# Chunk-selected attention with a gated linear unit: ten of the 32 query and key transposes moved from TensorE to DMA, and a new order

## The chip, the cores and the metric

One core of a Trainium2 chip runs the whole program. It has TensorE (matrix multiplications and transposes, into PSUM banks), VectorE, ScalarE and GpSimd for element-wise work, and SyncE (SP), which here only issues DMAs. The metric is the device time of one execution in microseconds (us); a kernel is told by the median of its runs. In the profile the engines are PE (PEld is its weight load), DVE, ACT, POOL and SP.

## The reference

The inputs are q, k and v of shape (4, 8, 768, 64), fp32, and three weights. Keys lie in 24 chunks of 32. For each query and each chunk an upper bound of the score is formed from the chunk's smallest and largest keys; the six best chunks among those not in the future are kept, and a causal softmax attention runs over them. A gated unit with a causal convolution of width 5 follows.

```python
k_min, k_max = np.min(k_chunks, axis=3), np.max(k_chunks, axis=3)
ub = np.sum(np.maximum(q[:, :, :, None, :] * k_min[:, :, None, :, :],
                       q[:, :, :, None, :] * k_max[:, :, None, :, :]), axis=-1)
ub = np.where(causal, ub, -1e9)
top_chunks = np.argsort(ub, axis=-1)[..., -6:]
scores = 0.125 * q @ k^T, masked to the chosen chunks and to pos_q >= pos_k
attn_out = softmax(scores) @ v
x = attn_out.transpose(0, 2, 1, 3).reshape(B, S, H * D)
gate = sigmoid(sum over j of conv_w[j] * x shifted by 4 - j)
out = (gate * (x @ w_val)) @ w_out
```

## The kernel before, in words

The 32 heads are worked as 16 pairs p (0 to 15); the two heads of a pair fill the 128 partitions with 64 each. Four pairs make one batch entry. Each step of a pair is a named operation in a graph; `build` (line 282) declares it with its engine, its assumed cost, what it reads and writes, and the PSUM groups it uses. The program isn't scheduled by the graph: the list `ORDER` (line 114) writes out all 1616 names in one order, with the PSUM bank after "=", and `emit_in_order` emits them so. Each engine executes its own operations strictly in that order, and so does each DMA queue; waits between engines follow from the data.

The names, for pair p and half w (384 of 768 positions):

- `Lk`, `Lq`, `Lv`: loads on SP (line 621). A key or query load is one DMA per head; pair 0 is split in two parts, so four DMAs each.
- `KT`, `QT`: three fp32 128x128 transposes on TensorE each (line 637). From PSUM, `KE` (ScalarE) casts the keys to fp16, `KX` (VectorE, four for a pair) takes maximum and minimum of each chunk, `QH` (ScalarE) casts the queries to fp16, times 16, and `QL` (VectorE) forms the fp16 rest.
- `AH`, `AL` (VectorE): |q| in two fp16 parts. `KB`, `KS` (GpSimd): the chunk bounds in fp16 parts. `KN` and `KM` don't exist before.
- `CF`, `BD` (TensorE): the bounds; `T8` (VectorE): the eight largest; `CM`: the mask; `MT` with `ME`: the mask turned on TensorE and copied, for pairs 0 to 9; `MD`: the same by one DMA transpose, for pairs 10 to 15. Pair 0 takes its bounds in fp32 instead (`KF`, `QF`, `RF`, `BF`), and all its five `BF` lie in one PSUM bank.
- `S` (TensorE): scores with the mask added; `E` (ScalarE): exp; `A` (GpSimd): the causal triangle; `VC` (GpSimd): values to fp16; `AV` (TensorE): times values; `RC`, `NR` (VectorE): normalisation.
- `XT`: the result turned for the second part, by DMA for pairs 8 to 14, by TensorE with `XTE` else; `XH` (GpSimd): the convolution's halo.
- `CV` (TensorE, for two pairs): convolution; `TH` (ScalarE): gate; `VL`, `GV`: x times w_val, times gate; `OU`, `OE`, `ST`: output matmul, eviction, store. `wval`, `wvd`, `wout` load the weights; `wvd` copies w_val to the other half of the partitions on SP's queue.
- `F`, `G`: filler matmuls at the start.

Line 640 is thus all fp32 transposes, 653 is `KX`, 647 `KE`, 682 `QH`, 721 `QL`, 728 and 731 `AH` and `AL`, 765 `BD`, 773 `T8`, 796 `MD`, 813 `S`, 838 `AV`, 862 `XT` by DMA, 902 `CV`, 917 `VL`, 923 `GV`, 931 `OU`, 939 `OE`.

Of the kernel before, what the change touches and what calls it, by code (L numbers as in the profile page):

```python
# [75 lines left out]
def emit_in_order(graph, names, nbanks=8):  # L76
# [24 lines left out]
    "dmat": set(range(8, 15)),  # L101
    "dmam": set(range(10, 16)),
# [12 lines left out]
mKF0 wval30 mfz F0=0 F1 F2 F3 F4 F5 mxT F6 F7 F8 ident identb mKB1 cfill identh mVA0 F9 F10 F11 F12  # L115
F13 Lq0.0 F14 F15 G14=1 G12 G13 G10 G11 G9 Lk0.0 KT0.0=2 KX0.00 KX0.01 QT0.0=3 G3 Lk0.1 KT0.1=4 G17
KX0.10 G6 G19 G5 RF0.0 KE0.0 G18 G7 G4 G16 KX0.11 G1 KF0.11 KF0.10 QF0.0 ident2 G2 KF0.00 KF0.01 G0
Lk1.0 KT1.0=5 KX1.01 KX1.00 KT1.1=6 KX1.11 mVA1 em0 em1 KX1.10 Lq0.1 QT0.1=7 G15 BF0.2=0 BF0.1 cwl
KE0.1 RF0.1 QF0.1 BF0.5 BF0.3 BF0.4 em2 QH0.1 Lq2.0 QT2.1=2 QT2.0=4 mNS0 mKB0 cwn1 T80.5 cwn0 cwt=7
# [59 lines left out]
E10.14 KX12.01 T811.3 S10.5=07 BD11.2 T811.2 T811.5 AV8.05 E10.05 KB12.5 AV8.03 E10.04 S10.3=54
E10.03 E10.15 E10.13 S10.0=60 E10.10 BD11.1 E10.00 AV8.00 A9.01 KB12.0 A9.03 A9.04 AV9.01=3 AV9.05  # L180
T811.4 KT13.1=5 T811.1 RC8.0 NR8.0 CM11 AV9.03 AV9.04 AV9.02 KX13.10 KX13.11 AV9.12=7 AV9.00 Lq13.0
RC9.0 NR9.0 S10.1=41 E10.11 KE13.1 AV9.10 AV9.15 E10.01 AV9.13 AV9.11 S10.2=02 E10.02 KT13.0=6
KX13.01 KX13.00 KE13.0 Lv10 wout2 VC10 E10.12 AV9.14 wvd1 MD11 CV3.0=1534 CV3.1 TH3.11 TH3.01 RC9.1
NR9.1 S11.4=06 E11.04 E11.14 AL12 VL0.0=72 GV0.01 GV0.00 A10.15 A10.03 S11.2=43 TH3.00 S11.0=06
# [55 lines left out]
def pool(n, per=0.86):  # L240
# [856 lines left out]
```

## Time and profile before

| | |
|---|---|
| median of 3 runs | 187.21 us (186.26 to 188.31) |
| profiled execution | 186.9 us, span 185.2 us |
| granted TensorE clock | 1.00 |
| busy: TensorE, ScalarE, VectorE, GpSimd | 176.5, 140.3, 125.8, 109.6 us |
| DMA queue of SP and ScalarE | 28.06 MB, 73.0% of 16 engines' span |

The span runs from the first to the last instruction. A busy share is an average over stages that have different limits. Matmuls are pipelined and their ends are modelled, so a full TensorE in a window of small matmuls needn't be full. In the rows, "x" is a count; in the groups of instructions the columns after the bar are busy time, mean duration of one in ns, and the idle time of the engine before them with what ended it. In windows, each engine's busy time is followed by its count of instructions, then the granted clock, the DMA share and GB/s. In the chain of waits the columns are start, duration, and what.

### The profile page before, as it was taken

The numbers are of one execution on the slowest core, as the hardware profiler recorded it, in microseconds if no ns is written. First come the engines' busy times: TensorE is split into PE (matmuls) and PEld (weight loads), VectorE is DVE, ScalarE is ACT, GpSimd is POOL, SyncE is SP. The second block draws the span as 40 slices with busy tenths as digits, with TensorE's granted clock in tenths as the row PEclk, the third lists the DMA queues.
The fourth block names the chain that finished last, engine by engine and source line by source line (L and its number), as shares of the span: only waits on it lengthen the run. The fifth ranks groups of instructions, "written<-read, shape, count | busy, mean of one in ns | idle before, by whom it ended". The sixth has DMA issues, their size and how long they took to land.

```text
span 185.2 us, 8893 instructions
## 1 busy us (share of the span) xinstructions
PE 176.5 (95%) x3714; PEld 127.2 (69%) x3714; DVE 125.8 (68%) x429; ACT 140.3 (76%) x320; POOL 109.6 (59%) x309
## 2 busy tenths in 40 slices
PE   7999999999999999989899999998999999999992
PEld 5696666878876787767667685786667677656441
DVE  0569999989999889998664579558923432710370
ACT  2369999999999799998698767595765979248032
POOL 7965899999999958899729423248641634100000
PEclk9999999999999999999999999999999999999999
DMA  5999989999999999960679993895047239537046
GB/s 106 213 221 217 204 189 231 193 192 229 195 210 190 211 217 199 226 122 4 144 133 178 183 209 98 178 98 151 4 81 90 69 95 173 153 119 282 8 173 224
DMA packets 89912, 29.68 MB, mean 160 GB/s; under 512 B 85387, under 2 KB 86667, under 8 KB 89872
## 3 DMA queue, kind: packets, MB, share of 16 engines
q1 hardware_dynamic: 88880, 28.06, 73.0%
q0 software_dynamic: 992, 1.06, 4.1%
q8 instruction: 29, 0.48, 1.1%
q14 instruction: 11, 0.09, 0.2%
HBM read 20.98 MB, written 6.29 MB: 147 GB/s over the span
## 4 chain that ended last, share of the span: by engine, by line
PE 59%; DVE 23%; DMA 7%; issue 3%; POOL 2%; ACT 2%; SPq 2%; DVEq 0%; POOLq 0%; ACTq 0%
PE ps L917 10%; PE ps L931 9%; DVE KK L653 8%; PE ps L902 7%; PE ps L838 7%; PE ps L810 6%; PE ps L640 6%; PE ps L813 5%; DMA vn<-in_v_dram 3%; PE ps L765 3%; DVE ON L848 3%; DVE TOP L773 3%; DMA xT<-ON 3%; DVE QL L721 2%; DVE RH L728 2%
## 5 line engine op out<-in xcount | busy, mean ns | idle before, releaser
L817 ACT ACTIVATE P<-ps 128x512 f16<-128x512 f32 (+1 forms) x192 | 89.6, 596 | 7.1 <-PE ps L813 6.6
L829 POOL TENSOR_SCALAR_AFFINE_SELECT P<-P 128x256 f16<-128x256 f16 (+1 forms) x128 | 43.6, 363 | 19.7 <-ACT P L817 18.2
L813 PE MATMUL ps<-QM,EM 64*128 64x512 f16 (+4 forms) x256 | 37.4, 290 | 0.3
L653 DVE TENSOR_REDUCE KK<-ps 128x12 f32<-128x384 f32 x64 | 32.8, 549 | 6.8 <-PE ps L640 6.4
L810 PE MATMUL ps<-QH,KE 64*128 64x512 f16 (+4 forms) x256 | 35.7, 291 | 0.0
L923 DVE SCALAR_TENSOR_TENSOR GV<-G,ps 128x384 f16<-128x384 f32 x32 | 16.3, 549 | 23.6 <-PE ps L917 23.6
L838 PE MATMUL ps<-VA,P 128*128 128x65 f16 x672 | 30.7, 194 | 0.9 <-DVE KK L653 0.6
L838 PEld LDWEIGHTS <-P 128*128 128x128 f16 x672 | 26.3, 98 | 6.5 <-issue 2.9
L917 PE MATMUL ps<-xT,wv 64*128 64x384 f16 x256 | 24.1, 323 | 0.5 <-issue 0.5
L939 ACT ACTIVATE OSB<-ps 128x512 f32<-128x512 f32 (+1 forms) x22 | 12.9, 597 | 15.0 <-PE ps L931 7.7
L931 PE MATMUL ps<-wo,GV 128*128 128x512 f16 (+1 forms) x100 | 22.9, 370 | 0.0
L773 DVE MAX8 TOP<-ps 128x8 f32<-128x16 f32 (+4 forms) x160 | 15.9, 166 | 8.3 <-PE ps L765 5.4
L907 ACT ACTIVATE G<-ps 128x384 f32<-128x384 f32 x32 | 14.0, 502 | 8.4 <-PE ps L902 8.3
L740 POOL CAST VA<-vn 128x768 f16<-128x768 f32 x16 | 14.3, 892 | 9.2 <-DMA vn<-in_v_dram 9.1
L917 PEld LDWEIGHTS <-wv 64*128 64x128 f16 x256 | 13.5, 94 | 8.8 <-issue 1.9
L647 ACT ACTIVATE KE<-ps 128x384 f16<-128x384 f32 x32 | 16.8, 564 | 2.3 <-DVE KK L653 1.5
L810 PEld LDWEIGHTS <-KE 64*128 64x128 f16 x256 | 14.0, 94 | 6.1 <-issue 1.6
L902 PE MATMUL ps<-xT,diag 32*32 32x384 f16 x1280 | 17.5, 326 | 0.6 <-issue 0.5
L848 DVE TENSOR_TENSOR ON<-ps,RCP 128x384 f16<-128x384 f32 x32 | 17.5, 553 | 0.7
L682 ACT ACTIVATE QH<-ps 128x384 f16<-128x384 f32 x32 | 15.7, 543 | 3.0 <-PE ps L640 3.0
L902 PEld LDWEIGHTS <-diag 32*32 32x32 f16 x1280 | 14.2, 88 | 3.4 <-issue 1.7
L640 PE MATMUL ps<-ident,kn 128*128 128x128 f32 x96 | 15.5, 281 | 0.3 <-DMA kn<-in_k_dram 0.3
(75 smaller groups left out, 305.7 us busy)
## 6 DMA issues: line engine op xcount, KB each, us to landing
vn<-in_v_dram SPq DMA_DIRECT2D x16, 384.0 KB, 6.3
out_dram<-OSB SPq DMA_DIRECT2D x23, 256.0 KB, 2.8
kn<-in_k_dram SPq DMA_DIRECT2D x30, 192.0 KB, 4.8
qn<-in_q_dram SPq DMA_DIRECT2D x30, 192.0 KB, 5.2
wv<-in_moe_w_val_dram POOLq DMA_DIRECT2D x8, 64.0 KB, 4.4
wo<-in_moe_w_out_dram POOLq DMA_DIRECT2D x4, 128.0 KB, 4.8
wv<-wv SPq DMA_DIRECT2D x4, 128.0 KB, 4.7
qn<-in_q_dram SPq DMA_DIRECT2D x4, 96.0 KB, 2.8
```

The source lines that it names most:

```text
L640: nc.tensor.transpose(out=pt[:, tl * 128:(tl + 1) * 128], in_=t[:, 3 * w + tl, :], identity=ident)
L653: nc.vector.tensor_reduce(out=KK[p % 2][:, mx, w * 12:(w + 1) * 12], in_=bank(gr, None).rearrange("p (c t) -> p c t", t=CH), axis=AX.X, op ...
L773: nc.vector.max(out=TOP[p % 2][:, it - 1, s, :], in_=bounds(gr)[:, it - 1, s * NCH:s * NCH + n])
L810: nc.tensor.matmul(out=pq[hh][:, col + a:col + n], lhsT=KE[p % 3][HP[hh], ks], rhs=QH[p % 3][HP[hh], q0 + a:q0 + n], start=True, stop=False)
L813: nc.tensor.matmul(out=pq[hh][:, col + a:col + n], lhsT=EM[HP[hh], ks], rhs=qm[HP[hh], q0 + a - 128:q0 + n - 128], start=False, stop=True)
L817: e.EX = lambda p, hh, bi, tot, gr: nc.scalar.activation(out=PT[hh, bi, p % 2][:, 0:tot], in_=bank(gr, None)[:, 0:tot], func=AF.Exp, scale ...
L829: nc.gpsimd.affine_select(out=ap, in_=ap, pattern=[[0, n], [1, 128]], compare_op=ALU.is_ge, fill=0.0, base=0, channel_multiplier=-1)
L838: nc.tensor.matmul(out=pav[:, qt, :], lhsT=PT[a, bi, p % 2][:, col:col + 128], rhs=VA[p % 3][:, hh, jt, :], start=(jt == 0), stop=(jt == qt))
L848: e.NR = lambda p, hh, gr: nc.vector.tensor_tensor(out=ON[(p // 2) % 2][:, 2 * (p % 2) + hh].rearrange("p t h d -> p h t d"), in0=bank(gr, ...
L902: nc.tensor.matmul(out=pc[i][os], lhsT=diag[rs, cp * NG + gi, j, :], rhs=x[rs, gi, :, a:a + 128], start=(j == 0), stop=(j == 2 * KSZ - 1), ...
L917: nc.tensor.matmul(out=pv[h], lhsT=wval_sb[HP[h], n, wc:wc + 255:2], rhs=xT[HP[h], (b % 2) * 2 + cp, gi, :, LD:LD + 128], start=(n == 0), ...
L931: nc.tensor.matmul(out=po[:, 0:z - a], lhsT=GVT[(b % 2) * NCT + et][:, s * 128:(s + 1) * 128], rhs=wout_sb[:, et, a:z], start=(et == 0), s ...
```

## The change

Four things are edited.

1. The first loads: each part of pair 0's keys and queries is issued as two DMAs of one head each on two queues, head 0 on SP (`Lk0.0` and so on), head 1 on ScalarE (`Hk0.0`).
2. The first bounds: pair 0's `BF` lie in three banks (tiles 5 and 4, 3 and 2, 1); its mask is turned in two pieces (`MT0`/`ME0` for tiles 2 to 5, `MU0`/`MV0` for tile 1). Two of the four `KF` go from ScalarE to VectorE.
3. The queries of pairs 10 to 15: `QN.0` (ScalarE) casts the loaded queries to fp16, `QN.1` (VectorE) forms the fp16 rest, and `QD.0` and `QD.1` turn both by DMA transposes on SP straight into `QH` and `QL`. `QT`, `QH` and `QL` are gone there. The keys of pairs 12 to 15: `KN.0` (ScalarE) casts, `KN.1` and `KN.2` (GpSimd) form the rest times 2048 in fp16, `KY.0` and `KY.1` turn both by DMA, `KN.3` (VectorE) adds them back to fp32, and two `KM` (VectorE) take the chunk bounds over 768 columns. `KT`, `KE` and `KX` are gone there. The fp16 parts use the memory of earlier tensors (`CW`, `QF`).
4. `ORDER` is another one (1610 names).

```diff
+    "dmaq": set(range(10, 16)),
+    "dmak": set(range(12, 16)),
...
+BGRP = {5: 0, 4: 0, 3: 1, 2: 1, 1: 2}
...
+                if nsp == 2:
+                    for hh, en in enumerate(("SP", "ACT")):
+                        g.op(en, 500, 500, "LH"[hh] + f"{what}{p}.{part}",
+                             lambda part=part, hh=hh, en=en: e.load(what, p, part, nsp, en, (hh,)), (),
+                             [(key, k4, part, "h")[:3 + hh]], dma=1800.0 / 4)
+                    continue
...
+    def QN(p, n):
+        hi, lo = QNA[:, p % 2, 0:S], QNA[:, p % 2, S:S + SELT * 128]
+        t = qn[p % 4]
+        if n == 0:
+            nc.scalar.activation(out=hi, in_=t.rearrange("p t d -> p (t d)"), func=AF.Copy, scale=QS)
+        else:
+            nc.vector.scalar_tensor_tensor(
+                out=lo, in0=t[:, 1:NT].rearrange("p t d -> p (t d)"), scalar=QS, in1=hi[:, 128:S],
+                op0=ALU.mult, op1=ALU.subtract)
+    def QD(p, n):
+        dst, src = (QL[p % 2], QNA[:, p % 2, S:S + SELT * 128]) if n else (QH[p % 3], QNA[:, p % 2, 0:S])
+        nc.sync.dma_start_transpose(out=dst.rearrange("p (t c) -> p t c", c=128), in_=src)
+    def KN(p, n):
+        t = kn[p % 4].rearrange("p t d -> p (t d)")
+        hi, lo, lot = KNA[:, 0], KNA[:, 1], KNA[:, 2]
+        if n == 0:
+            nc.scalar.activation(out=hi, in_=t, func=AF.Copy)
+        elif n == 1:
+            nc.gpsimd.tensor_tensor(out=t, in0=t, in1=hi, op=ALU.subtract)
+        elif n == 2:
+            nc.gpsimd.tensor_scalar(out=lo, in0=t, scalar1=LS, scalar2=None, op0=ALU.mult)
+        else:
+            nc.vector.scalar_tensor_tensor(out=t, in0=lot, scalar=1.0 / LS, in1=KE[p % 3],
+                                           op0=ALU.mult, op1=ALU.add)
+    def KY(p, n):
+        dst, src = (KNA[:, 2], KNA[:, 1]) if n else (KE[p % 3], KNA[:, 0])
+        nc.sync.dma_start_transpose(out=dst.rearrange("p (t c) -> p t c", c=128), in_=src)
+    e.KMx = lambda p, mx: nc.vector.tensor_reduce(
+        out=KK[p % 2][:, mx], in_=kn[p % 4].rearrange("p t (c i) -> p (t c) i", i=CH), axis=AX.X,
+        op=ALU.min if mx else ALU.max)
```

The new order of the parts that the prediction speaks of, by engine (names of other steps left out where marked):

```
SP, start:  Lk0.1 Lk0.0 Lk1.0 Lq0.1 Lq0.0 Lk2.0 Lq1.0 Lq2.0 Lk3.0 ...
ACT queue:  Hq0.0 Hq0.1 Hk0.1 Hk0.0, ahead of the first KE
VectorE, start: KX0 (4) KX1.11 KF0.11 KF0.01 KX1.00 KX1.01 T80.4 KX1.10 KX2.01 KX2.00 T80.5 KX2.11 CM0.5 T80.3 T80.2 CM0.4 CM0.3 CM0.2 KX2.10 QL1.0 T80.1 ME0 ...
SP, later:  ... QD10.0 QD11.1 Lv9 QD10.1 Lq12.0 QD11.0 Lk14.0 Lk13.0 MD10 wvd1 KY12.0 KY12.1 wvd2 wvd0 wvd3 MD11 Lq13.0 QD12.0 KY13.0 KY13.1 QD12.1 QD13.0 QD13.1 Lv10 KY14.0 KY14.1 Lq14.0 MD12 Lk15.0 Lv11 QD14.0 ST0.0 QD14.1 MD13 XT10 Lv12 KY15.0 XT11 KY15.1 XT9 XT8 MD14 ...
GpSimd:     ... wval30 KB11.3 ... A10.04 A10.15 wout0 XH7 KN13.1 KN13.2 A10.03 KB12.0 KB12.5 KB12.1 wout3 wout2 ...
TensorE:    ... CV3 VL0.0 S11.1 VL0.3 S11.5 S11.2 S11.3 VL0.1 S11.0 S11.4 VL0.2 CV7 OU0.5 OU0.0 CF12 BD12 (5) OU0.4 OU0.2 OU0.1 AV10.12 ...
```

More of the change, by code (lines that the diff above doesn't have):

```diff
@@ L114 @@
 ORDER = """
[L115 to L119, printed above, removed]
@@ L179 @@
[L179 to L184, printed above, removed]
@@ L185 @@
-TH3.10 VL0.1=12 GV0.10 E11.10 E11.00 S11.1=57 E11.01 Lk14.0 AH12 A10.14 E11.02 E11.11 A10.11 Lq14.0
-GV0.11 VL0.2=60 GV0.20 GV0.21 E11.12 KB12.1 S11.3=15 E11.13 VL0.3=24 S11.5=76 E11.05 E11.03 KS12
-KB12.2 VC11 KB12.4 A10.01 KB13.0 A10.04 A11.14 GV0.30 CF12=3 KB13.5 KB12.3 BD12.2 BD12.4 BD12.5
-KB13.1 BD12.3 T812.3 A10.13 KS13 XT7=0 XTE7 XH7 A10.05 KB13.2 KT14.1=5 KX14.10 GV0.31 T812.5 KB13.3
-QT13.1=7 QH13.1 Lv12 QL13.1 E11.15 A11.15 Lv15 QT14.0=2 QT13.0=1 QT14.1=0 KT14.0=6 KX14.01 QH13.0
-QL13.0 AL13 BD12.1 T812.2 QH14.1 QH14.0 AH14 QL14.0 KE14.0 KE14.1 Lk15.0 KB13.4 Lq15.0 AV10.05=4
@@ new lines @@
+AV9.10 AV9.14 AV9.11 KY12.0 KN13.0 CM11 A9.15 AV9.15 RC9.0 NR9.0 S10.0=35 RC9.1 NR9.1 KY12.1 KN12.3
+KM12.0 wvd2 wvd0 KM12.1 CV3.0=2104 E10.10 E10.00 wvd3 CV3.1 TH3.00 TH3.11 TH3.01 VL0.0=76 GV0.01
+GV0.00 wout1 MD11 S11.1=53 E11.01 E11.11 VL0.3=24 GV0.31 TH3.10 GV0.30 QN12.1 S11.5=06 E11.05 E11.15
+S11.2=57 E11.12 S11.3=31 E11.13 E11.03 VL0.1=04 GV0.10 GV0.11 Lq13.0 QN13.0 QN13.1 A10.04 A10.15
+QD12.0 AH12 E11.02 wout0 S11.0=62 E11.10 E11.00 S11.4=71 XH7 VL0.2=30 CV7.0=5426 CV7.1 KY13.0 KN13.1
@@ new lines @@
+KN14.0 KN13.2 A10.03 KY13.1 KN13.3 GV0.20 KB12.0 KB12.5 KB12.1 wout3 GV0.21 TH7.10 TH7.00 QD12.1
+wout2 OU0.5=3 TH7.11 TH7.01 OE0.5 A11.03 A10.14 QD13.0 QN15.0 AL12 OU0.0=0 KM13.0 KM13.1 A11.13
+OE0.0 KS12 KB12.2 E11.14 A10.13 KB12.4 CF12=4 KB12.3 BD12.4 BD12.2 BD12.1 KN14.1 KN14.2 BD12.5
+BD12.3 T812.3 OU0.4=5 OE0.4 OU0.2=6 OE0.2 OU0.1=2 OE0.1 KB13.0 KB13.5 A10.01 KB13.1 AH13 QD13.1 AL13
+Lv10 VC10 AV10.12=3 AV10.02=0 AV10.13 KS13 KB13.2 KY14.0 KB13.3 A10.05 OU0.3=1 CF13=5 KB13.4 T812.2
+T812.1 T812.5 AV10.10 BD13.2 BD13.5 BD13.3 AV10.14 T812.4 CM12 OE0.3 AV10.01 E11.04 KY14.1 KN14.3
@@ L309, in pair @@
         load("v", "vn")
-        for w in range(2):
+        if p in P["dmak"]:
+            knk = [("kn", k4, 0), ("kn", k4, 1)]
+            over = [(x, 0, w) for x in ("QF", "RF") for w in range(2)] if p == min(P["dmak"]) else []
+            c, l = act(S)
+            g.op("ACT", c, l, f"KN{p}.0", lambda: e.KN(p, 0), knk, [("KNh",)] + over, ())
+            c, l = pool(S)
+            g.op("POOL", c, l, f"KN{p}.1", lambda: e.KN(p, 1), knk + [("KNh",)], knk, ())
+            g.op("POOL", c, l, f"KN{p}.2", lambda: e.KN(p, 2), knk, [("KNl",)] + over, ())
+            g.op("SP", 1300, 1300, f"KY{p}.0", lambda: e.KY(p, 0), [("KNh",)],
+                 [("KE", k3, w) for w in range(2)], (), dma=700.0)
+            g.op("SP", 1300, 1300, f"KY{p}.1", lambda: e.KY(p, 1), [("KNl",)], [("KLO",)] + over, (),
+                 dma=700.0)
+            c, l = dve(S)
+            g.op("DVE", c, l, f"KN{p}.3", lambda: e.KN(p, 3),
+                 [("KLO",)] + [("KE", k3, w) for w in range(2)], knk, ())
+            for mx in range(2):
+                g.op("DVE", c, l, f"KM{p}.{mx}", lambda mx=mx: e.KMx(p, mx), knk,
+                     [("kk", k2, mx, w) for w in range(2)], ())
+        for w in range(2) if p not in P["dmak"] else ():
             gr = g.group()
             g.op("PE", 3 * 109, 2 * 109 + 280, f"KT{p}.{w}", lambda w=w, gr=gr: e.KT(p, w, gr),
-                 [("kn", k4, w), ("ident",)], [("kps", p, w)], [gr])
+                 [("kn", k4, w), ("kn", k4, w, "h"), ("ident",)], [("kps", p, w)], [gr])
             c, l = act(HB)
@@ L336, in pair @@
                 for n in range(2):
[L337 removed]
+                    eng = "DVE" if n else "ACT"
+                    g.op(eng, 90, 205, f"KF{p}.{hh}{n}", lambda hh=hh, n=n: e.KFb(p, hh, n), kks,
                          [("KF", k2, hh, n)], ())
@@ L381, in pair @@
              [("VA", k3)], ())
-        gr = g.group()
+        gs = [g.group() for _ in range(3 if full else 1)]
+        bg = {it: gs[BGRP[it] if full else 0] for it in range(1, NT)}
         for it in range(1, NT):
+            gr = bg[it]
             if full:
@@ L619, with load @@
     cq = {"k": (kn, k), "q": (qn, q), "v": (vn, v)}
-    def load(what, p, part, nsp, eng):
+    def load(what, p, part, nsp, eng, heads=(0, 1)):
         en = nc.sync if eng == "SP" else nc.scalar
@@ L629, in load @@
         n = NT // nsp
-        for hh in range(2):
+        for hh in heads:
             en.dma_start(
```

268 lines of the change are left out of this document (150 added, 118 removed).

## The prediction

> **What bounds the kernel now.** I read the busy time in long stretches first, then TensorE's transposes in the same stretches.
>
> ```profile
> core 0: us, PE busy (x) PEld busy (x) DVE busy (x) ACT busy (x) POOL busy (x), PEclk, DMA share, GB/s
> 0.00:20.00 20.00, 18.39 (x182) 13.90 (x183) 12.01 (x50) 12.25 (x30) 14.22 (x39) 1.00 1.10 191
> 20.00:95.00 75.00, 72.65 (x1569) 55.31 (x1568) 68.31 (x245) 70.80 (x167) 64.83 (x181) 1.00 0.94 185
> 95.00:105.00 10.00, 9.80 (x273) 6.69 (x274) 6.05 (x15) 7.80 (x17) 7.09 (x19) 1.00 0.79 144
> 105.00:180.00 75.00, 74.16 (x1689) 50.38 (x1684) 39.05 (x122) 48.04 (x107) 23.45 (x71) 1.00 0.55 125
> ...
> 95.00:105.00 10.00, 0.90 (x6) 0.42 (x5) 1.00 0.79 144
> 105.00:180.00 75.00, 3.64 (x30) 3.24 (x30) 1.00 0.55 125
> ```
>
> The first rows are all instructions by engine; the last two are line 640 alone, TensorE's fp32 transposes of keys and queries. There are three regimes. To 20 us VectorE and ScalarE are idle two fifths of the time, so the stretch waits for first data. From 20 to 95 us ScalarE (70.8 of 75) and VectorE (68.3) are nearly full, and TensorE's 72.65 is flattering, because the modelled ends of its small matmuls cover the gaps. From 105 to 180 us TensorE is busy 74.2 of 75 while VectorE has 39 and ScalarE 48: there TensorE is the bound. The granted clock is 1.00 throughout.
>
> The chain of waits agrees, and shows one place where it leaves TensorE.
>
> ```profile
> 109.07 1.97 PE ps L640 x18
> ...
> 113.40 0.86 PE ps L931 x4
> ...
> 116.05 0.61 SPq L862
> ...
> 116.72 5.96 DMA vn<-in_v_dram
> ...
> 127.26 0.31 PE ps L765 x6
> ```
>
> Eighteen transposes of pairs 13 and 14 stand on the chain for 1.97 us, 0.109 us each; four output matmuls take 0.86. From 116 to 127 us the chain runs through SP's queue and a load of values that was issued late, then GpSimd, and TensorE filled that time with other work.
>
> **The change part by part, against the profiled execution of 186.9 us (span 185.2, 1.7 around it); the median of the three runs is 187.2.** With the spread of those runs, about 1% is what a measurement can tell from no change.
>
> *Transposes taken off TensorE.* Queries of six pairs (QT 10 to 15) and keys of four (KT 12 to 15), six transposes each: 60 x 0.109 = 6.6 us. Pairs 13 to 15 run after 95 us: 6 + 30 = 36 in the two rows above, 36 x 0.109 = 3.9 us out of the stretch that TensorE bounds. The other 24 (2.6 us) run before 95 us, where TensorE isn't the bound; I count nothing for them by themselves.
>
> *What replaces them on the other engines.*
>
> ```profile
> L817 ACT ACTIVATE P<-ps 128x512 f16<-128x512 f32 x160 | 84.6, 653 | 3.8 <-PE ps L813 3.5
> L817 ACT ACTIVATE P<-ps 128x128 f16<-128x128 f32 x32 | 8.4, 310 | 3.3 <-PE ps L813 3.1
> L647 ACT ACTIVATE KE<-ps 128x384 f16<-128x384 f32 x32 | 16.8, 564 | 2.3 <-DVE KK L653 1.5 <-DVE RCP L844 0.7
> L682 ACT ACTIVATE QH<-ps 128x384 f16<-128x384 f32 x32 | 15.7, 543 | 3.0 <-PE ps L640 3.0
> L653 DVE TENSOR_REDUCE KK<-ps 128x12 f32<-128x384 f32 x64 | 32.8, 549 | 6.8 <-PE ps L640 6.4 <-ACT KE L647 0.4
> L721 DVE SCALAR_TENSOR_TENSOR QL<-ps,QH 128x384 f16<-128x384 f32 x15 | 8.2, 550 | 0.8 <-ACT QH L682 0.8
> L721 DVE SCALAR_TENSOR_TENSOR QL<-ps,QH 128x256 f16<-128x256 f32 x15 | 6.1, 411 | 0.1
> L740 POOL CAST VA<-vn 128x768 f16<-128x768 f32 x16 | 14.3, 892 | 9.2 <-DMA vn<-in_v_dram 9.1
> L1054 POOL TENSOR_TENSOR diag<-ident,cw 128x320 f16<-128x320 f16 x8 | 5.8, 722 | 0.0
> ```
>
> ScalarE: L817 gives (653 - 310) / 384 = 0.89 ns an element, so one cast of 768 (QN.0, KN.0) is about 0.88 us, where two evictions of 384 took 1.09 (QH) or 1.13 (KE). All ten pairs: -12 x 0.543 - 8 x 0.564 + 10 x 0.88 = -2.2 us. VectorE: L721 gives 1.09 ns an element, so QN.1 (640) is 0.83 us against 0.96 for the two QL; a minimum or maximum over 768 (KM) is about 0.95, KN.3 about 0.97, so a pair's keys cost 2.87 instead of 4 x 0.549 = 2.20. In all -6 x 0.13 + 4 x 0.67 = +1.9 us. No row shows these forms. The nearest that reads SBUF is RH:
>
> ```profile
> L728 DVE TENSOR_SCALAR RH<-QH x15: 317/320/1908, 16.5 to 127.7; 128x640 uint16<-128x640 uint16 x15
> ```
>
> It took 0.32 us for 640 and once 1.91. From below the 18 new VectorE instructions would then cost about half of my prices; from above, each 1.1 us more, 20 us, of which 16 are late, where VectorE has 36 us of 75 free. I keep the slopes, since these are fp32 operands as in L721.
>
> What counts is where they fall. Before 95 us VectorE loses QL 10 to 12 and KX 12 (2.9 + 2.2 us) and gets QN.1 of pairs 10 and 11 (1.7) and XTE7 (about 0.6): 2.8 us less. ScalarE loses six QH and two KE (4.4) and gets four casts (3.5): 0.9 less. The rest of the keys of pair 12 stands in the new order behind CM11, beside TensorE's bound. With the two QN.1 there at 1.91 each VectorE's relief shrinks to 0.6. The stretch, held by both engines, gives 0.6 to 2.8; I take 1.5, nearer ScalarE's figure since that engine is fuller.
>
> GpSimd gets KN.1 and KN.2 four times: a 768-wide cast took 0.89 us; 320 elements of two inputs took 0.72, which would be 1.73 at 768. I take 1.5 + 0.9, 9.6 us in all, from 95 us on, where it is busy 30.5 of 85. That is off the path unless something stands behind it: KB12, the last two loads of the output weights (wout3, wout2, before the first OU), and KY13.1.
>
> *Twenty transposes more on SP's queue.*
>
> ```profile
> L862 SPq DMA_TRANSPOSE xT<-ON x7: 1212/1667/4510, 108.7 to 159.7; - x7
> ...
> DMA to landing us min/median/max: 2.7/4.1/7.5
> ...
> L796 SPq DMA_TRANSPOSE QM<-NS x6: 1200/1243/1712, 87.7 to 140.8; - x6
> ...
> DMA to landing us min/median/max: 2.6/2.6/4.1
> ...
> vn<-in_v_dram SPq DMA_DIRECT2D x16, 384.0 KB, 6.3
> ```
>
> Undisturbed, a transpose holds SP 1.2 us and lands after 2.6; among loads it held SP 4.5 and landed after 7.5. Twenty are 24 us of SP, whose waits in the second half are long, and a share of the DMA engines that are 0.55 busy there. So a query that was ready about a microsecond after its matmul now comes 3.8 us after its cast (1.2 + 2.6) at best, 12 at worst; the order gives it that lead, since QD10 to QD15 stand far ahead of their S. The lead is thin in three places, where TensorE works in order and can't pass: VL0.0 needs wvd3, behind MD10 and the two transposes KY12; BD12 needs QD12.1, behind KY13.1, which itself waits for two GpSimd instructions; AV10 needs Lv10, now behind eight transposes and followed directly by its cast. Each can be late by nothing or by 7.5 - 2.6 = 4.9 us. I count 1.5, the lower third of one such place, as the undisturbed rows are the usual ones.
>
> The Trainium skill ("VectorE: DVE Perf Modes", "The three transpose paths") gives 390 ns for a 128x128 transpose on TensorE and 1309 ns through the DMA crossbar, and its "Rules for kernel authors" send it to TensorE where a PSUM destination will do, which speaks against this change. By that figure six blocks would be 7.9 us, an estimate from that page, and the thin places would be missed each time, as in the last rival below; here five blocks landed in 2.6 us and TensorE took 0.109 a block, so the measurement decides and the sum keeps its 1.5.
>
> *First loads by head, first bounds in three banks.*
>
> ```profile
> 0.79 1.28 ACT L700 ACT_TABLE_LOAD   x1 [0.79 <-PEq L1081]
> 0.80 0.98 SPq L631 DMA_DIRECT2D qn<-in_q_dram  x2
> 1.83 3.52 SPq L631 DMA_DIRECT2D kn<-in_k_dram  x6
> 5.99 1.02 DVE L653 TENSOR_REDUCE KK<-ps 128x12 f32<-128x384 f32 x2 [4.79 <-PE ps L640]
> 6.67 0.52 PE L640 MATMUL ps<-ident,kn 128*128 128x128 f32 x3 [0.27 <-DMA kn<-in_k_dram]
> 9.32 0.52 PE L640 MATMUL ps<-ident,qn 128*128 128x128 f32 x3
> 9.81 0.62 PE L713 MATMUL ps<-KF,QF 128*128 128x48 f32 x4
> 12.43 0.91 DVE L773 MAX8 TOP<-ps 128x8 f32<-128x24 f32 x10 [1.49 <-PE ps L713]
> 14.01 0.45 PE L790 MATMUL ps<-identh,NS 128*128 128x128 f16 x5
> ...
> kn<-in_k_dram SPq DMA_DIRECT2D x4, 96.0 KB, 3.1
> ```
>
> SP spends about 0.5 us an issue. The last key half of pair 0 is its sixth issue and reaches TensorE at 6.67. With keys first on SP and the other head on ScalarE's queue (third and fourth there), it is issued at about 2.3 and landed, after 3.1, at 5.4 to 5.9; all queries by about 6.4, where QT0.1 ran at 9.32. VectorE's four reductions (0.51 apart) then end near 7.6 instead of 8.2, and BF0.4 can start near 8.6 instead of 9.81. The maxima no longer wait for the fifth BF (12.43), since each bank has its own reader. But VectorE gets the reductions of pairs 1 and 2 ahead of MT0, some 6 us of work behind 8.5, so MT0 isn't earlier; what is won is idle time of VectorE between 6 and 20 us, of which there are 2.0 (14.0 less the 12.0 busy in the first row above). Bounds 0 to 2.0. No row shows an issue on ScalarE's queue: if its table load (1.28) went ahead of the four issues, the last key half would land after 6.7 and the start would lose about 1. I take 1.0.
>
> The sum: 3.9 + 1.5 + 1.0 - 1.5 = 4.9; 186.9 - 4.9 = **182.0 us**.
>
> **The rivals.** *All is collected*: no thin place is missed, and start and front give their upper bounds. 3.9 + 2.8 + 2.0 = 8.7, so 178.2. For it: TensorE at 74.2 of 75; against it: every new chain must keep its time.
>
> *The value load is the bound.* The chain above left TensorE for eleven microseconds over a late value load; Lv10 to Lv15 are still issued late, between transposes. If they hold AV10 to AV15, the 3.9 us aren't collected: 1.5 + 1.0 - 1.5 = 1.0 remains, 185.9. Against it: TensorE had other work during those eleven microseconds.
>
> *Slower: SP's queue holds each of the last four pairs.* KY waits at the head of the queue for GpSimd's KN.2, and everything behind it (QD, MD, value loads, stores) waits with it. If BD or AV of pairs 12 to 15 comes late each time by half of the 4.9, that is 9.8 us: 186.9 - 6.4 + 9.8 = 190.3. It turns into a loss above 6.4 / 4 = 1.6 us a pair. For it: 4.51 us in one SP transpose; against it: GpSimd is a third busy there, so KN.2 should be early.
>
> **How the numbers follow.** Forecast 0.48 (own range 180 to 184.5); all collected 0.15 (177 to 180); value load 0.25 (184 to 187.8); SP's queue 0.12 (187.5 to 193). A range of 178.0 to 187.6 leaves out about 0.05 below and 0.12 above. Faster by over 1% is below 185.3: 0.48 + 0.15 + 0.08 of the third = 0.71; within 1%: 0.17 of the third and 0.02 of the last = 0.19; slower 0.10.
>
> **What would show it.** Line 640's transposes fall from 192 to 132, none after 105 us; transposes on SP from 13 to 33, median landing near 3 us; the last 80 us of the span keep TensorE full but begin about 2.5 us earlier and are about 4 shorter. The first maxima come near 9 us instead of 12.43. Wrong would be: gaps of over 1 us on TensorE ahead of VL0, BD12 or AV10 with a DMA as releaser; ScalarE reloading a table or idle at the start; new casts that take over 1.1 us.

## The result, and the profile after

The change made the kernel slower, by 1.2%: less than 2%, but clear of the noise. Its median over 20 runs is 188.58 us (186.88 to 189.68) against 186.44 us for the kernel before on the same chip; the ratio is 1.0118 with a 95% interval of 1.0091 to 1.0144. Forecast were 182.0 us, a range of 178.0 to 187.6 and a chance of 0.10 for slower. The profiled execution took 188.21 us (span 186.5, 1.3 more than before).

First the same stretches as before, all instructions by engine, and one more, 80 to 120 us, which turned out to be the one that matters.

```profile
core 0: us, PE busy (x) PEld busy (x) DVE busy (x) ACT busy (x) POOL busy (x), PEclk, DMA share, GB/s
0.00:20.00 20.00, 16.28 (x131) 12.71 (x131) 11.05 (x40) 9.79 (x24) 12.29 (x36) 0.91 1.17 196
20.00:95.00 75.00, 71.69 (x1615) 54.96 (x1612) 66.48 (x251) 70.96 (x164) 68.19 (x178) 1.00 1.00 182
105.00:180.00 75.00, 70.52 (x1631) 45.39 (x1627) 44.41 (x119) 46.91 (x98) 40.62 (x92) 1.00 0.91 169
80.00:120.00 40.00, 33.77 (x904) 22.46 (x902) 27.82 (x76) 30.76 (x66) 35.79 (x72) 1.00 1.16 163
```

Before, 80 to 120 us read so:

```profile
80.00:120.00 40.00, 38.39 (x983) 27.81 (x981) 28.24 (x91) 30.65 (x71) 22.80 (x66) 1.00 0.70 135
```

In these 40 us TensorE lost 4.6 us of busy time, GpSimd went from 22.8 to 35.8 (nine tenths busy) and the DMA share from 0.70 to 1.16. The transposes that left account for all of TensorE's loss: they were busy for 5.6 us there before and for 0.5 after. What they freed stood idle, and other work didn't move up into it. From 105 us on TensorE is no longer full: 70.5 of 75, where it had 74.2. The work did leave TensorE: 132 fp32 transposes are left of 192, the last at 80.6 us.

```profile
L690 PE MATMUL ps<-ident,kn x72: 272/273/424, 6.3 to 80.6; 128*128 128x128 f32 x72
L690 PE MATMUL ps<-ident,qn x60: 272/273/308, 11.1 to 66.3; 128*128 128x128 f32 x60
```

Over the whole span TensorE's busy time fell by 5.4 us (176.5 to 171.1) while the span grew by 1.3, so it stood idle 6.7 us longer. The chain of waits shows the two places (columns: start, duration, what). The start:

```profile
2.42 5.15 DMA kn<-in_k_dram
7.71 0.85 PE ps L690 x3
8.56 2.13 PE ps L1044 x10
10.70 1.60 PE ps L690 x12
...
13.52 0.04 DVE TOP L868
```

The last key half of pair 0 is the fourth issue on ScalarE's queue; it lands at 7.6 us, ten filler matmuls stand on the chain, then the twelve transposes include pair 1's keys, which the new order puts ahead of pair 0's queries. The first maxima (L868) come at 13.5 us; before they came at 12.43. In the middle, the first row is pair 12's `KN.2` on GpSimd, which stands on the chain itself; the rest is the place that is followed below.

```profile
81.12 2.13 POOL QF L814
...
105.19 7.05 DMA QL<-CW
...
112.27 0.80 DVE RL L784
113.07 1.74 DVE KK L826 x2
...
114.88 0.84 POOL KD L713 x2
...
116.56 0.86 POOL VA L835
...
119.75 0.61 PE ps L860 x18
```

At 105 us the transpose of pair 12's query rests (`QD12.1`) takes 7.05 us to land. VectorE works in order: `AL12` (L784) waits for it, the two `KM13` (L826) wait behind `AL12`, GpSimd's `KB13` waits for those, the value cast `VC10` (L835) waits behind the first steps of `KB13` in GpSimd's order, and TensorE gets `AV10` and `BD13` at 117 to 120 us. The transposes' issues and landings, and what VectorE's `AH` and `AL` waited for:

```profile
QH<-CW SPq DMA_TRANSPOSE x6, 4.9
QL<-CW SPq DMA_TRANSPOSE x6, 5.4
QM<-NS SPq DMA_TRANSPOSE x6, 3.5
KE<-QF SPq DMA_TRANSPOSE x4, 5.0
QF<-QF SPq DMA_TRANSPOSE x4, 3.5
```

```profile
L784 DVE SCALAR_TENSOR_TENSOR RL<-QH,QL 128x320 uint32<-128x320 uint32 x15 | 9.4, 624 | 6.0 <-DMA QL<-CW 5.9
L781 DVE TENSOR_SCALAR RH<-QH 128x640 uint16<-128x640 uint16 x15 | 7.6, 506 | 2.5 <-DMA QH<-CW 2.5
```

VectorE stood 8.4 us for them. The medians to landing are 3.5 to 5.4 us, not about 3, and the mask's own transpose (`QM<-NS`), 2.6 before, now takes 3.5. (The transposes of the results, `xT<-ON`, didn't get later: 4.1 before, 3.6 now.) Last, GpSimd's new steps (min, median and max in ns):

```profile
L814 POOL TENSOR_SCALAR QF<-kn x4: 2128/2130/2485, 81.1 to 129.4; 128x768 f16<-128x768 f32 x4
```

```profile
L812 POOL TENSOR_TENSOR kn<-kn,QF x4: 1639/1644/1647, 78.0 to 127.7; 128x768 f32<-128x768 f32 x4
```

`KN.2` takes 2.13 us where the sum had 0.9; `KN.1` takes 1.64 where it had 1.5.

### The profile page after: what moved, and what is told of

Same layout as the page of the kernel before. It is cut to its first block, busy times and chain, and to the rows that moved or that the text cites. A ratio compares the mean times of both kernels' runs of the same rounds, so it can differ in the third digit from the quotient of the medians.

```text
span 186.5 us, 8827 instructions
## 1 busy us (share of the span) xinstructions
PE 171.1 (92%) x3654; PEld 120.8 (65%) x3654; DVE 130.5 (70%) x422; ACT 138.5 (74%) x308; POOL 129.8 (70%) x317
## 4 chain that ended last, share of the span: by engine, by line
PE 35%; POOL 26%; ACT 14%; DMA 9%; SPq 5%; issue 4%; DVE 3%; ACTq 1%; POOLq 0%
ACT P L912 10%; PE ps L1012 9%; POOL P L924 7%; DMA QL<-CW 7%; PE ps L1026 6%; PE ps L933 5%; POOL VA L835 4%; PE ps L997 3%; DMA kn<-in_k_dram 3%; PE ps L905 3%; POOL QF L814 2%; POOL KB L723 2%; PE ps L860 2%; PE ps L908 2%; PE ps L690 2%
## 5 line engine op out<-in xcount | busy, mean ns | idle before, releaser
L924 POOL TENSOR_SCALAR_AFFINE_SELECT P<-P 128x256 f16<-128x256 f16 (+1 forms) x128 | 46.0, 382 | 9.3 <-ACT P L912 7.8
L908 PE MATMUL ps<-QM,EM 64*128 64x512 f16 (+4 forms) x256 | 36.4, 289 | 0.0
L905 PE MATMUL ps<-QH,KE 64*128 64x512 f16 (+4 forms) x256 | 34.5, 291 | 0.0
L933 PE MATMUL ps<-VA,P 128*128 128x65 f16 x672 | 29.1, 193 | 1.4 <-POOL VA L835 1.4
L933 PEld LDWEIGHTS <-P 128*128 128x128 f16 x672 | 25.0, 97 | 6.7 <-issue 3.5
L703 DVE TENSOR_REDUCE KK<-ps 128x12 f32<-128x384 f32 x48 | 24.2, 548 | 6.1 <-PE ps L690 4.6
L1018 DVE SCALAR_TENSOR_TENSOR GV<-G,ps 128x384 f16<-128x384 f32 x32 | 16.3, 549 | 10.9 <-PE ps L1012 9.2
L868 DVE MAX8 TOP<-ps 128x8 f32<-128x12 f32 (+4 forms) x160 | 16.2, 165 | 6.0 <-PE ps L860 5.7
L905 PEld LDWEIGHTS <-KE 64*128 64x128 f16 x256 | 13.5, 94 | 6.5 <-issue 2.1
L835 POOL CAST VA<-vn 128x768 f16<-128x768 f32 x16 | 14.6, 912 | 2.8 <-DMA vn<-in_v_dram 2.5
L860 PE MATMUL ps<-KB,RH 128*128 128x48 f16 x150 | 13.4, 183 | 3.0 <-POOL KB L723 2.5
L697 ACT ACTIVATE KE<-ps 128x384 f16<-128x384 f32 x24 | 12.2, 543 | 5.2 <-PE ps L690 4.3
L1026 PEld LDWEIGHTS <-GV 128*128 128x128 f16 x100 | 8.8, 97 | 10.9 <-issue 1.6
```

The costliest lines, as they stand in the source:

```text
L703: nc.vector.tensor_reduce(out=KK[p % 2][:, mx, w * 12:(w + 1) * 12], in_=bank(gr, None).rearrange("p (c t) -> p c t", t=CH), axis=AX.X, op ...
L835: nc.gpsimd.tensor_copy(out=o, in_=i)
L860: nc.tensor.matmul(out=o, lhsT=lt, rhs=KB[i2][:, j, :], start=False, stop=(n == 5), skip_group_check=True)
L905: nc.tensor.matmul(out=pq[hh][:, col + a:col + n], lhsT=KE[p % 3][HP[hh], ks], rhs=QH[p % 3][HP[hh], q0 + a:q0 + n], start=True, stop=False)
L908: nc.tensor.matmul(out=pq[hh][:, col + a:col + n], lhsT=EM[HP[hh], ks], rhs=qm[HP[hh], q0 + a - 128:q0 + n - 128], start=False, stop=True)
L924: nc.gpsimd.affine_select(out=ap, in_=ap, pattern=[[0, n], [1, 128]], compare_op=ALU.is_ge, fill=0.0, base=0, channel_multiplier=-1)
```

## The experiments

Ratios are to the kernel before on the same chip, with their 95% interval.

**Undoing a part.** Three kernels gave the transposes of the keys, of the queries, or of both back to TensorE, with each step put into the order at the earliest place that its inputs and buffers allow.

```diff
-    "dmak": set(range(12, 16)),
+    "dmak": set(),
...
+ KT12.0 KX12.00 KX12.01 KE12.0 KT12.1 ...  (into ORDER; likewise QT, QH, QL of 10 to 15 with "dmaq" empty)
```

> The changed kernel (188.6 us) with the keys of pairs 12 to 15 turned by TensorE again; queries stay on DMA, start and order stay. Theory: the late stretch loses its saving to GpSimd, which KN.1 and KN.2 hold for 3.8 us at a time (1.64 + 2.13), ahead of the KB, VC and weight loads that TensorE waits for; taking them away gives about 186.5 to 187.5 although TensorE gets 24 transposes (2.6 us) back. Rival (the keys cost nothing, the order or the start is at fault): 190 to 191, the 2.6 us on top.

> The changed kernel with the queries of pairs 10 to 15 turned by TensorE again; keys stay on DMA. Theory (GpSimd's part is the larger one, late QL transposes the smaller): the holes ahead of BD12, BD14 and BD15 go (together 2.4 us in the trace), 36 transposes (3.9 us) come back: 188.5 to 190. Rival (the late query transposes are the loss): 186 to 187.

> The changed kernel with no query or key turned by DMA beyond before: what is left of the change is the start and the order. Theory: TensorE has all its work again, but no late transfers and a free GpSimd: 187 to 189, the start's loss of up to 2 over the kernel before. Rival (the order itself is bad): 191 to 193, the 60 transposes (6.6 us at 0.109) largely on top.

Measured: 1.063 (1.0553 to 1.0708), 1.0662 (1.0598 to 1.0727) and 1.1621 (1.1553 to 1.1689), that is 198.8, 198.9 and 216.8 us, far outside every theory and rival above. These runs say nothing about the parts. In the chain of waits of the keys' run the transposes that were put back take turns with their own evictions:

```profile
111.01 0.49 PE ps L690 x3
...
112.11 1.03 DVE KK L703 x2
...
113.28 0.53 PE ps L690 x3
```

In that run 8.8 us of TensorE's waiting ended with VectorE's reductions (L703). The three runs measure their placement in an order that was made for other work. From here on parts were left out or shortened in place, so that the order of everything else stayed.

**GpSimd's scaling step alone.** `KN.2` is left out; `KN.1` writes the unscaled difference as fp16.

```diff
-LS = 2048.0
+LS = 1.0
...
-            nc.gpsimd.tensor_tensor(out=t, in0=t, in1=hi, op=ALU.subtract)
+            nc.gpsimd.tensor_tensor(out=lo, in0=t, in1=hi, op=ALU.subtract)
```

> The changed kernel without the scaling step on GpSimd: the subtraction writes its fp16 difference unscaled, KN.2 (2.13 us, four times) is left out, so the small parts of the keys of pairs 12 to 15 lie in fp16's lowest range. Theory (GpSimd's chain makes TensorE wait at BD10, AV8, BD11, AV10, BD13; 4.2 us of holes in the trace): 185.5 to 187. Rival (those holes would be filled by the next late thing, the query transposes): 188 to 188.6, as before this edit.

Measured 1.0116 (1.007 to 1.0161): no change from 1.0118. The theory that GpSimd's longer chain is the cause by itself falls.

**The new transposes alone.** All twenty are left out; their readers take what lies in the buffers.

```diff
- QD10.0 QD10.1 ... QD15.1  KY12.0 KY12.1 ... KY15.1   (out of ORDER)
-            nc.vector.scalar_tensor_tensor(out=t, in0=lot, scalar=1.0 / LS, in1=KE[p % 3],
+            nc.vector.scalar_tensor_tensor(out=t, in0=lo, scalar=1.0 / LS, in1=KE[p % 3],
```

> The changed kernel without its twenty new DMA transposes: the casts stay, but nothing is turned, and the readers take what an earlier pair left in the same buffers (KN.3 reads GpSimd's rest directly). Leaving out the scaling on GpSimd had changed nothing (188.4), so GpSimd's time is no longer the theory. Theory now: the late stretch loses its saving to the transposes themselves, by their landing (4.9 us in the median for QH and QL instead of 2.6) and by the other transfers that they hold up; without them 183 to 185.5. Rival (the new order, its start included, is slow by itself): 187.5 to 188.6.

Measured 1.0008 (0.9967 to 1.005), 1.1% below the kernel after, and still none of the gain. This edit takes out more than the transposes: the scores and bounds no longer wait for the loads and casts ahead of the queries' transposes either. So what the kernels without transposes gain is the price of the transposes and of these waits together.

**The start.** Pair 0 goes first: all its keys and queries on SP ahead of pair 1's, keys first on ScalarE's queue, and `QT0` ahead of `KT1`.

```diff
- Lk0.1 Lk0.0 Lk1.0 Lq0.1 Lq0.0 Lk2.0 ...   Hq0.0 Hq0.1 Hk0.1 Hk0.0
+ Lk0.1 Lk0.0 Lq0.1 Lq0.0 Lk1.0 Lk2.0 ...   Hk0.1 Hk0.0 Hq0.1 Hq0.0
```

> The changed kernel with its first loads on two queues as they are, but pair 0's keys and queries ahead of pair 1's keys on SP, keys ahead of queries on ScalarE's queue, and QT0 ahead of KT1.1 on TensorE. Theory (pair 1's keys, 384 KB, share the DMA engines with pair 0's second half, so the first scores come at 17.7 us instead of 14.7, and ScalarE, full from 20 us on, never makes up for it): first scores near 15, time 185.5 to 187. Rival (the start is made up for by 70 us, as the scores of pair 7 at 67.6 against 66.6 suggest): 188 to 188.6.

Measured 1.001 (0.997 to 1.0051), also 1.1% below after. The first maxima come at 10.7 us (13.5 in after, 12.4 in before) and the first scores at 15.4 (17.7 in after, 14.7 in before), near the theory's 15. A second kernel has this start with all eight loads on SP's queue, and a third is the kernel before with head 1's four loads on ScalarE's queue and nothing else changed.

```diff
-                    for hh, en in enumerate(("SP", "ACT")):
+                    for hh, en in enumerate(("SP", "SP")):
```

> The same with all eight first loads on SP alone, by head, keys first. Theory (the issues on ScalarE's queue cost nothing of their own, what counts is what shares the engines): within 0.7 us of the kernel with two queues, first scores 0.5 to 1 later. Rival (ScalarE's queue itself is slow: its keys landed after 4.7 us, SP's after 2.7): 1 us faster than the kernel with two queues.

> The kernel before (186.1 to 186.4) with one part of the change alone: head 1 of pair 0's four first loads is issued on ScalarE's queue, queries' first half first, the order else as it was. Theory: the last key half is issued about 1 us earlier; the start gains 0 to 1 us: 185.2 to 186.4. Rival (two queues share the engines, so everything lands later): 187 to 188.

Measured 1.0103 (1.0037 to 1.017) and 0.998 (0.9943 to 1.0018). Against the 1.001 above, the second queue is worth about 0.9% where the new order asks for keys and queries early, and this difference is uncertain by 0.8%; on the order of before it is worth nothing that can be told.

**Two and three at a time.** The same edits together, the second with the transposes left out too.

> Two edits together: the start with pair 0 first (alone 1.1% faster than the changed kernel) and GpSimd without the scaling step (alone without effect). Theory (several late things stand behind each other: taking one away uncovers the next, so GpSimd's time shows only when the others are early too): 185 to 186.3. Rival (GpSimd's time is truly slack): 186.8, as with the start alone.

> The same, and without the twenty new DMA transposes (nothing is turned, readers take what an earlier pair left). Theory (start, GpSimd and transposes hide the saving together): all 6.6 us of TensorE's time that the change removes minus what the front can't use, 182 to 184. Rival (the new order itself loses it in the stretch that VectorE and ScalarE bound): 185 to 186.5.

Measured 1.0026 (0.9985 to 1.0067) and 0.9758 (0.9715 to 0.9801). Taking two things out gave nothing more than one; taking all three gave 2.4% below the kernel before, 4.5 us. That left open which of them hold the gain, so the missing corners were run: pair 0 first without the transposes but with `KN.2`, and after's own start without either.

> The kernel after with pair 0 first and the twenty new DMA transposes left out, GpSimd's scaling step kept. If that step is a limit of its own once the start and the transposes are out of the way: 0.988 (0.982 to 0.996). If GpSimd matters only through the transposes that wait for it: as with all three out, 0.976 (0.970 to 0.980).

> The kernel after with GpSimd's scaling step and the twenty new DMA transposes left out, in after's own order of the start. With pair 0 first as well the ratio was 0.976. If the start is a serial delay that the later part cannot hide, as its 1.1% on the kernel after says, 0.987 (0.983 to 0.991). If a later wait swallows it, 0.976 to 0.980.

| ratio to before | with `KN.2` | without `KN.2` |
|---|---|---|
| after's start, transposes | 1.0118 | 1.0116 |
| after's start, no transposes | 1.0008 | 0.9791 (0.9721 to 0.9861) |
| pair 0 first, transposes | 1.001 | 1.0026 |
| pair 0 first, no transposes | 1.0028 (0.9995 to 1.006) | 0.9758 |

Either one, `KN.2` or the transposes, holds nearly the whole gain by itself; only without both does it show. The start costs about 1% in the two rows with the transposes and nothing that can be told in the others. The chains show why, at the same place. Pair 0 first, no transposes, `KN.2` kept:

```profile
108.27 1.63 POOL kn L803
...
109.97 2.27 POOL QF L805
...
112.31 1.21 POOL KD L704 x2
...
114.36 0.86 POOL VA L826
...
116.94 0.61 PE ps L851 x18
```

Pair 0 first, no `KN.2`, transposes kept:

```profile
79.91 5.51 DMA QH<-CW
...
85.71 4.80 DMA QM<-NS
...
101.79 5.40 DMA QF<-QF
...
110.09 1.73 DVE KK L825 x2
...
116.91 0.61 PE ps L859 x18
```

And with all three out:

```profile
106.33 1.74 DVE KK L815 x2
...
113.00 0.61 PE ps L849 x18
```

The last row of each is the same piece of work, 18 matmuls of `BD13`. It comes at 116.94 by GpSimd's own queue (`KN14.1` and `KN14.2`, 3.9 us, stand ahead of `KB13`'s first step and of `VC10`), at 116.91 by the landing of transposes, and at 113.00 without either. Two chains of the same length run side by side; shortening one leaves the other. In after itself they meet 0.9 us apart: GpSimd was through `KN14.2` at 114.0 us and then waited 0.85 us for VectorE's `KM13`, which stood behind the late transpose. For 80 to 120 us the rows without the transposes, with `KN.2` and without:

```profile
80.00:120.00 40.00, 33.76 (x954) 23.08 (x923) 28.98 (x78) 30.09 (x66) 34.80 (x71) 1.00 0.56 102
```

```profile
80.00:120.00 40.00, 37.73 (x998) 25.79 (x971) 31.33 (x90) 32.36 (x71) 31.95 (x78) 1.00 0.57 107
```

TensorE gets 4.0 us back there, close to the 5.0 us between the ratios 1.0028 and 0.9758.

**What of the transposes costs.** With pair 0 first and `KN.2` out, all twenty were issued at their places, but into buffers that nobody reads; and of the two kinds one was kept at a time.

```diff
+    DUM = ct_([128, 4, S], F16, "DUM")
...
-        dst, src = (QL[p % 2], ...) if n else (QH[p % 3], ...)
+        dst = DUM[:, DSL[f"QD{p}.{n}"], 0:SELT * 128 if n else S]
```

> The kernel after with pair 0 first and GpSimd's scaling step left out, and all twenty new DMA transposes issued at their places but into four buffers of their own that nobody reads; the scores and KN.3 read what lies in the old places. Theory of waiting (what costs is that the readers stand until a transpose has landed): as with the transposes left out, ratio 0.976 (0.970 to 0.985). Rival, congestion (what costs is that SP's queue and the DMA engines are held, so that value and weight loads behind them come late): as with the transposes read, 1.003 (0.995 to 1.010). Halfway, 0.985 to 0.995: both.

> The kernel after with pair 0 first, GpSimd's scaling step left out, the queries' twelve DMA transposes kept and read, and the keys' eight left out (the sum on VectorE reads the buffer of differences directly and old keys). Theory that the keys' transposes hold SP's queue, since they stand there behind GpSimd's work: 0.976 to 0.983. Rival, the queries' transposes, which the bounds read: 0.995 to 1.005.

> The kernel after with pair 0 first, GpSimd's scaling step left out, the keys' eight DMA transposes kept and read, and the queries' twelve left out (scores and bounds read old queries). Theory that the keys' transposes hold the queue: 0.995 to 1.005. Rival, the queries' ones: 0.976 to 0.983. Both together at 0.985 to 0.992 with the former kernel: each gives a part.

Measured: unread 0.9933 (0.9884 to 0.9981), queries only 0.9886 (0.9831 to 0.9941), keys only 0.9845 (0.9782 to 0.9908). Of the 2.7% between 0.9758 and 1.0026, 1.7% are there when nobody waits for the new transposes, and 0.9% come with the reading, which is also waiting for the loads and casts ahead of them. Each kind costs a part: 1.3% for the twelve of queries, 0.9% for the eight of keys; what is left, 0.5%, is less than these intervals can tell, and each of the shares is itself uncertain by 0.6 to 0.8%. The congestion can be seen on the old transposes of the mask: 3.7 us to landing with the unread ones, 2.6 without. On those of the results it can hardly be seen: 3.5 against 3.3.

**Two tries at a cure.** In one, `MD10` goes ahead of two key loads on SP's queue, and `Lv10` and its cast go forward; in the other ten loads leave SP's queue for ScalarE's. Both have pair 0 first and no `KN.2`.

```diff
- Lk14.0 Lk13.0 XT7 MD10 ...  KY13.0 KY13.1 wout3 QD12.1 wout2 QD13.0 QD13.1 Lv10 ...
+ XT7 MD10 Lk13.0 Lk14.0 ...  MD11 Lv10 Lq13.0 ...
```

> The start with pair 0 first, GpSimd without the scaling step, all transposes in, and two moves: MD10 ahead of the loads Lk13 and Lk14 on SP's queue, Lv10 right behind MD11 with its cast ahead of wout3 on GpSimd. Theory (what TensorE waits for at S10 and AV10 is a transfer that stands behind others on SP): the holes there (0.9 and 0.9 to 2.5 us in the traces) go, 184 to 185.5. Rival (the next late thing takes over): no change against the kernel without the moves.

```diff
-    "lq": {},
+    "lq": {(w, p): "ACT" for w, ps in (("k", (13, 14)), ("v", range(10, 16))) for p in ps},
```

> The kernel after with pair 0 first and the scaling step left out (differences cast unscaled), all transposes kept, and the key loads of pairs 13 and 14 and the value loads of pairs 10 to 15 issued on ScalarE's queue at their old places. If the congestion is that of SP's queue (a load or transpose standing behind 1.2 us of another transpose's issue): 0.985 to 0.994. Rival, the DMA engines themselves are held, or ten issues of 0.5 us on ScalarE eat the gain: 1.000 to 1.012.

Measured 1.0043 (1.0003 to 1.0083) and 1.0912 (1.0844 to 1.098). Neither helps, and no kernel here that does the whole computation beat the one before. The second doesn't tell the queue's order from the DMA engines, since it made another wait:

```profile
110.15 2.61 PE ps L1025 x12
...
112.78 0.01 ACT OSB L1033
112.79 5.61 DMA vn<-in_v_dram
...
118.46 0.86 POOL VA L834
...
119.36 0.71 PE ps L932 x10
```

`Lv10` stood behind an output eviction (L1033) in ScalarE's order, which waited for TensorE's output matmuls; the load was issued at 112.8 us and `AV10` began at 119.4. So what of the 1.7% is SP's order and what the DMA engines stays open.

**The kernel before with three pairs' queries by DMA.** Pairs 13 to 15 only, in the order of before.

```diff
+    "dmaq": {13, 14, 15},
...
+ QN13.0 QN13.1 QD13.0 QD13.1   (ahead of Lk14.0; likewise for 14 and 15)
```

> The kernel before (186.1 to 186.9) with only the queries of pairs 13 to 15 cast and turned by DMA, in the order of before, six transposes more on SP, 18 fewer on TensorE in the stretch that it bounds. Theory of the prediction's sum (TensorE's time in that stretch counts in full unless a transfer is late): -2.0 us, 184.3 to 185.3. Rival (the stretch is held by chains that TensorE only fills): within 0.7 us of the kernel before.

Measured 1.0973 (1.0885 to 1.1061).

```profile
122.31 1.25 ACT G L939 x3
123.56 1.17 SPq L976
...
124.83 3.27 DMA QM<-NS
```

TensorE's scores of pair 12 wait until 128.1 us for the mask's transpose, which is issued at 124.8 us behind an output store (L976) that waited for ScalarE. Over the run TensorE stood 8.8 us for two of these transposes, about half of what was lost. An order in which every engine works its list through is not changed in one place without moving all others; this run, like the first three, prices the place and not the part.

## Why the prediction was wrong

**The saving was about right, the cover was not.** 3.9 us from TensorE's late stretch and 1.5 from relief before it were counted, 5.4 together; with both chains out of the way 4.5 us (0.9758) show with pair 0 first and 3.9 (0.9791) with after's own start. The term that failed is the 1.5 us for "one thin place", together with GpSimd's new steps, which were taken to be off the path at no cost; the two chains took back 4.7 us. By the table the transposes take back 2.7% (5.0 us) with pair 0 first and `KN.2` out, and `KN.2` takes back as much where the transposes are gone. The three thin places that were named were the right ones in two cases: `BD12` waited 1.0 us for `AL12` and so for its transpose, and `AV10` behind its cast; `VL0.0` didn't wait. The sign that was named for them, a gap of over 1 us on TensorE with a DMA as releaser, never came: the gaps were 1.0 and 0.9 us, and VectorE and GpSimd ended them, since the late DMA stood one step or more further back. But the places were priced as chances of being late, by 2.6 us as the usual landing, when that figure came from transposes of the mask that ran where the DMA share was 0.34 to 0.70 (windows of 5 to 7 us around each of the six). The change itself raised that share to 1.16 in the stretch and the landing to 3.5 to 5.4, once 7.05, and four of the twelve query transposes held VectorE. With these terms the sum reads 186.4 - 4.5 + 4.7 (1.001 less 0.9758, both chains) + 2.0 (the start, against pair 0 first) = 188.6. It has to come out, because the terms are measured ratios laid end to end; it shows their sizes and is no check of them.

The Trainium skill, "VectorE: DVE Perf Modes", "The three transpose paths", gave by its figure an estimate of 7.9 us for six blocks, which the prediction set aside for the undisturbed 2.6. The longest landing on the chain, 7.05 us for five blocks, is above the 6.5 us that this figure would give for five (an estimate from that page), and most landings lie between 2.6 us and these estimates. The rule of that page's "Rules for kernel authors", TensorE where a PSUM destination will do, is what the kernel before follows for these blocks, and it is the faster of the two.

**GpSimd was read in the wrong window.** "A third busy there" was 30.5 of 85 us from 95 us on. But `KN.1` and `KN.2` of pairs 12 to 14 run from 78 to 115 us, where GpSimd was already 22.8 of 40 busy before (80 to 120 us), and they cost 3.8 us a pair instead of the 2.4 of the sum, most of it `KN.2` (2.13 instead of 0.9). It became nine tenths busy, with the bounds' chain and the value casts behind those steps in its order. The text named what stands behind them (`KB12`, the weights, `KY13.1`) and took them to be off the path; the output matmuls also waited 0.5 us for the weights.

**The start** was to gain 1.0 us; in its place it cost up to 1.1% (2.0 us) against the start with pair 0 first, and the first scores came 3.0 us later than in before. The bound of minus 1 was for ScalarE's table load going first; it didn't (the first issue is at 0.79 us). The four issues on that queue were late for another reason: keys stood third and fourth there, and pair 1's key transposes stood ahead of pair 0's queries. The maxima were to come near 9 us and came at 13.5.

**The rivals.** The slower one, SP's queue holding the last pairs, had the right place and the right sign with 0.12; its 190.3 assumed 9.8 us, and 4.7 were lost. The mechanism that it named shows little: in after's trace SP stood at `KY` 1.1 us for `KN.2`, 2.9 us for GpSimd in all, while late landings held VectorE for 8.4 us and GpSimd's steps held its own later work. "Value load the bound" named `AV10`, which did wait, but for GpSimd's order, not for the load. Right were the sizes on VectorE and ScalarE. The rows:

```profile
L792 ACT ACTIVATE CW<-qn 128x768 f16<-128x768 f32 x6 | 5.2, 862 | 1.0 <-DMA QH<-CW 1.0
L794 DVE SCALAR_TENSOR_TENSOR CW<-qn,CW 128x640 f16<-128x640 f32 x6 | 5.0, 835 | 0.0
L826 DVE TENSOR_REDUCE KK<-kn 128x24 f32<-128x768 f32 x8 | 7.2, 946 | 0.1
L816 DVE SCALAR_TENSOR_TENSOR kn<-QF,KE 128x768 f32<-128x768 f16 x4 | 4.1, 1015 | 2.5 <-DMA QF<-QF 2.5
```

Forecast and then measured, in us: casts 0.88 and 0.86; `QN.1` 0.83 and 0.84; `KM` 0.95 and 0.95; `KN.3` 0.97 and 1.02. Right too were 132 transposes on TensorE and 33 on SP. Two prices were wrong, `KN.2` (0.9 and 2.13) and the landing (2.6 and 3.5 to 5.4); the rest of the failure lay in who waits for an operation.

## What to carry to other kernels

When work moves from a full engine to "idle" ones, read the receivers' busy time in the stretch where the moved steps will run, not in a long average, and take a transfer's landing time at the load that the change will make, not as it was before. In a schedule of in-order queues ask for each moved step what stands behind it on its engine; two chains of equal length hide each other, so take both out together before calling either harmless. An undo that puts steps back into a foreign order measures the order.

## What the hardware showed

- GpSimd's multiplication by a constant from fp32 to fp16, 768 elements wide, took 2.13 us, more than the subtraction of two inputs, fp32 and fp16, of the same width (1.64) and well over the cast of the same width (0.91, L835). The Trainium skill, "GPSIMD Engine Reference", "4.1 Engine selection", has one-input operations at about line rate there; the trace doesn't agree for this form.
- With pair 0 first and no `KN.2`, the DMA share in 80 to 120 us was 0.57 without the twenty new DMA transposes, 1.07 with them unread and 1.16 with them read. The median landing of the mask's transposes, which the change didn't touch, went from 2.6 to 3.7 and 3.8 us; that of the results' stayed at 3.2 to 3.5.
- The granted TensorE clock was 0.91 in the first 20 us of after's profile, where TensorE was busy for 16.3 us, and 1.00 with pair 0 first, where it was busy for 17.4. No run separates the clock's part in the start's cost from the waiting.
